# Cross-covariance attention and channel mix on one core: q's root and spread two to three k pieces later in the head, the gated loads one k piece sooner

## The chip, the cores and the metric

The kernel runs on one core of a Trainium2 chip. The time is the device time of one execution in microseconds. It was 508.25 us before the change, the median of four runs (507.77 to 508.81).

## What is computed

Four batches of q, k and v, each 6208 rows by 256 channels in fp32, go through a cross-covariance attention and then through a channel mix. All norms run over the rows, so the attention matrix is only 256 by 256 for each batch:

```
qn = q / (norm(q, axis=1) + 1e-6);  kn = k / (norm(k, axis=1) + 1e-6)
a  = softmax(kn^T @ qn / tau)            # 256 x 256 per batch
x  = v @ a
xk = mu_k * x + (1 - mu_k) * shift(x);   xr = mu_r * x + (1 - mu_r) * shift(x)
out = sigmoid(xr @ w_r) * (relu(xk @ w_k)^2 @ w_v)
```

Here shift moves x down by one row within its batch; w_k is 256 by 1024, w_v 1024 by 256, w_r 256 by 256.

## The kernel before, in words

The 6208 rows of a batch are cut into NB = 12 pieces of 512 rows and a rest of 64 rows (piece 12). The order of all work on every engine is the order in which the program writes it down: each engine takes its own instructions in that order, and an instruction that has to wait holds up all that stand behind it on that engine. DMAs that SyncE (SP) issues form one queue, those that GpSimd (POOL) issues another; the latter also cast fp32 to bf16.

**The head** handles batch 0 alone. The list `order` (L554 to L557) puts q pieces 0 to 7, then q's rest, then k pieces 0 to 3 in turn with q pieces 8 to 11, then k's rest (g = 12), then k pieces 4 to 9; L578 to L582 add k pieces 10 and 11 in halves and quarters.

- A q piece (L125) is loaded by SP, cast to bf16 on DVE (L130), squared on ACT (L132), and PE sums the squares into `nq_ps` (L115), one piece late through `pend` and `flush`. Filler matmuls (L194) follow.
- A k piece (L138) is loaded by SP into one of eight `f` buffers, cast on DVE (L143) into one of six `kb` buffers, squared on ACT (L145), multiplied with the q piece of the same rows into the covariance `s_ps0` on PE (L148, eight matmuls), and then the norms of the piece before are flushed.
- When q's sums are complete, which is behind k's rest, `root` (L154) copies `nq_ps` out of PSUM on DVE (L159) and POOL raises it to the power one half (L161). `inverse` (L164) and `spread` (L173) are six small DVE operations; `broadcast` (L182) is six small matmuls that put q's inverse norms along the free axis of every partition (`bc_ps`). A DVE copy (L570) keeps them as `rq_bc0`. They are used only behind the last k piece (L590), when the softmax of batch 0 begins.
- The loads of later work wait at a gate: POOL copies one column of a k piece's bf16 tile (L572), which has to wait for that piece's cast; behind it on POOL stand the loads of v block 0 (`v_load(0)`, L234), w_k (L574), v blocks 1 and 2, and the first q and k rows of batch 1 (L432).

Which step stands behind which k piece is set by four conditions in the loop over `order`:

```python
            if g == NB:
                nq = root(nq_ps, 2)
            if g == NB - LEAD + 1:
                bc_ps = broadcast(spread(inverse(nq, 2)), "v", bufs=2)
            if g == 8:
                nc.vector.tensor_copy(rq_bc0, bc_ps)
            if g == 8:
                nc.gpsimd.tensor_copy(gate, kt[:, 0, 0:1])
                v_load(0)
```

With NB = 12 and LEAD = 8 these stand behind k's rest, k5, k8 and k8.

**Behind the head** comes k's own root, the softmax of batch 0, PE transposes of v block 0 (L254), fillers, and `x_first` (L269): the matmuls of x for block 0 (`x_ps`, L275), then the PE transposes of v block 1, which need that block's load.

**The body** (L629) runs over 49 blocks of 512 rows in eight steps each. A step holds the up projection of one block (L339, with ACT's relu at L343 and DVE's square at L350), the down projection of the block before (L399), the gate matmuls (L360), x of a later block (L265), the mixing (L307, L318), and a share of the covariance of the next batch (L443, L447, L475 to L487), whose loads POOL issues (L432).

Of the kernel before, what the change touches and what calls it, by code (L numbers as in the profile page):

```python
# [18 lines left out]
def kernel(  # L19
# [21 lines left out]
    NB = N // M  # L41
# [40 lines left out]
    def rows_of(g):  # L82
        return (P, S) if g < NB else (L, 1)
# [5 lines left out]
    LEAD = 8  # L89
# [35 lines left out]
    def q_piece(g, last=False):  # L125
        rows, n = rows_of(g)
        f = head_load(q, 0, g, 0, n)
        qt = pq.tile([P, S, C], BF16, name="qb", tag="b2", bufs=NB + 1)
        qb[g] = qt
        nc.vector.tensor_copy(qt[:rows, :n], f[:rows, :n])  # L130
        sq = pq.tile([P, S, C], BF16, name="hsq", tag="hsq", bufs=5)
        nc.scalar.activation(sq[:rows, :n], f[:rows, :n], AF.Square)  # L132
        flush()
        pend.append((nq_ps, "q", sq, rows, n, last))
        if g < NB:
            filler(FQ, g)

    def k_piece(g, s0, s1, last=False):  # L138
        rows, n = rows_of(g)
        n = s1 - s0  # L140
        f = head_load(k, 0, g, s0, s1)
        kt = pq.tile([P, S, C], BF16, name="kb", tag="kb", bufs=6)
        nc.vector.tensor_copy(kt[:rows, :n], f[:rows, :n])  # L143
        sq = pq.tile([P, S, C], BF16, name="hsq", tag="hsq", bufs=5)
        nc.scalar.activation(sq[:rows, :n], f[:rows, :n], AF.Square)  # L145
        for s in range(n):
            for ih in range(2):
                nc.tensor.matmul(s_ps0[:, ih, :], kt[:rows, s, ih * P:(ih + 1) * P], qb[g][:rows, s0 + s, :],  # L148
                                 start=first("s"), stop=last and s == n - 1, skip_group_check=True)
        flush()  # L150
        pend.append((nk_ps, "k", sq, rows, n, last))
        return kt

    def root(src, n):  # L154
        a = pn.tile([P, 4], F32, name="nrm_a")
        if len(src.shape) == 3:
            nc.vector.tensor_reduce(a[:, :n], src, axis=AX, op=OP.add)
        else:
            nc.vector.tensor_copy(a[:, :n], src)  # L159
        r = pn.tile([P, 4], F32, name="nrm_r")  # L160
        nc.gpsimd.tensor_tensor(r[:, :n], a[:, :n], half[:, :n], op=OP.pow)  # L161
        return r

    def inverse(r, n):  # L164

        nc.vector.tensor_scalar_add(r[:, :n], r[:, :n], 1e-6)
        o = pn.tile([P, 4], F32, name="nrm_o")
        nc.vector.reciprocal(o[:, :n], r[:, :n])
        return o
# [3 lines left out]
    def spread(r):  # L173
        w = pn.tile([P, 3, 2], BF16, name="rw", bufs=1)
        d = pn.tile([P, 2], F32, name="rd", bufs=1)
        nc.vector.tensor_copy(w[:, 0], r[:, :2])
        nc.vector.tensor_tensor(d, r[:, :2], w[:, 0], op=OP.subtract)
        nc.vector.tensor_copy(w[:, 1], d)
        nc.vector.tensor_tensor(w[:, 2], d, w[:, 1], op=OP.subtract)
        return w  # L180

    def broadcast(w, tag, **kw):  # L182
        bc_ps = ps.tile([P, 2, P], F32, name="bc_ps", tag=tag, **kw)
        for h in range(2):
            for u in range(3):
                nc.tensor.matmul(bc_ps[:, h], w[:, u, h:h + 1].to_broadcast([P, P]), ident,
                                 start=h == 0 and u == 0, stop=u == 2, skip_group_check=True)
        return bc_ps.rearrange("p h d -> p (h d)")

    def filler(n, src=0):  # L190

        f_ps = ps.tile([P, M], F32, name="f_ps", tag="v", bufs=2)
        for u in range(n):
            nc.tensor.matmul(f_ps, ident, qb[src].rearrange("p s c -> p (s c)")[:, :M], start=u == 0, stop=u == n - 1)  # L194
# [36 lines left out]
    def v_load(i):  # L231
        b, t = blocks[i]
        v_bf = pq.tile([P, S, C], BF16, name="v_bf", tag="b2", bufs=NB + 1)
        nc.gpsimd.dma_start(v_bf, v[b, t * M:(t + 1) * M, :].rearrange("(s p) c -> p s c", p=P))  # L234
        st[i, "v"] = v_bf
# [312 lines left out]
    def more_rows(n):  # L548
        while pos["load"] < min(len(loads), n):
            group_load(*loads[pos["load"]])  # L550
            pos["load"] += 1
# [6 lines left out]
    for what, g in order:  # L558
        if what == "q":
            q_piece(g, last=g == NB - 1)  # L560
        else:
            kt = k_piece(g, 0, rows_of(g)[1])
            if g < NB - LEAD or g == NB:
                filler(2 if g < NB else 3)
            if g == NB:
                nq = root(nq_ps, 2)
            if g == NB - LEAD + 1:
                bc_ps = broadcast(spread(inverse(nq, 2)), "v", bufs=2)
            if g == 8:
                nc.vector.tensor_copy(rq_bc0, bc_ps)  # L570
            if g == 8:
                nc.gpsimd.tensor_copy(gate, kt[:, 0, 0:1])  # L572
                v_load(0)
                nc.gpsimd.dma_start(w_k_sb, moe_w_k.rearrange("(ko ki) f -> ki ko f", ki=P))  # L574
                v_load(1)
                v_load(2)
                more_rows(1)
# [51 lines left out]
    for i in range(-2, NBLK):  # L629
        for j in range(8):  # L630
# [61 lines left out]
            for u in due.get(T, []):  # L692
                b, g, s = units[u]
# [48 lines left out]
```

## Time and profile before

| | us |
|---|---|
| median of four runs | 508.25 |
| the profiled execution | 507.97 |
| its span, first to last instruction | 506.2 |
| ACT busy | 430.5 |
| POOL busy | 105.2 |

The granted clock of TensorE was 1.000 of full speed. The page gives the busy time of each engine, the span in 40 slices, and the chain of work that ended last. The head fills the first three slices and a little more: up to 38 us the DMA engines move 320 to 387 GB/s, behind it about 200. By the chain, PE carries 82% of the span, DMA 7% and DVE 6%. In rows of time the columns are start, length, engine, line, operation, tiles, shapes and count, and in brackets the idle time before it and what ended that. A row of the chain has start, length, engine, tile and line. A row of windows has the stretch, its length, the busy time (and number) of PE, PE's weight loads, DVE, ACT and POOL, the clock, the share of the DMA engines and GB/s.

### The profile page before, as it was taken

What the parts mean: (1) busy time and instruction counts of PE and PEld (TensorE: products, weight loads), DVE (VectorE), ACT (ScalarE), POOL (GpSimd) and SP (SyncE); (2) the same over time, 40 slices, a digit from 0 to 9 for tenths busy, and PEclk for the clock granted to TensorE, in tenths of its full rate; (3) what the DMA queues carried; (4) which work ended last, traced back from release to release, by engine and by line L of the source; (5) the groups of instructions that cost most, each with busy time, mean ns of one, the idle gap of its engine ahead of it and who ended that gap; (6) DMA issues with size and microseconds to landing.
All of it is one profiled execution on the core that took longest, in us unless ns stands there. A gap on an engine that the chain in (4) does not pass through costs nothing.

```text
span 506.2 us, 9690 instructions
## 1 busy us (share of the span) xinstructions
PE 490.2 (97%) x3644; PEld 339.3 (67%) x3707; DVE 447.6 (88%) x706; ACT 430.5 (85%) x809; POOL 105.2 (21%) x145
## 2 busy tenths in 40 slices
PE   5799999999999999999999999999999999999997
PEld 2474677777676676676677666767666666666675
DVE  3468798999999999999999999999998788887875
ACT  6787999999998998998999899898787777777774
POOL 0047523332521221221342132100121000000000
DMA  8999999999999999899699999953298753424123
GB/s 332 387 320 192 184 202 206 203 208 197 178 165 205 191 196 142 136 171 169 120 179 196 176 199 154 152 130 83 62 155 163 148 103 93 98 76 91 44 84 105
DMA packets 143535, 83.48 MB, mean 165 GB/s; under 512 B 51264, under 2 KB 140032, under 8 KB 143488
## 3 DMA queue, kind: packets, MB, share of 16 engines
q0 software_dynamic: 65808, 33.01, 53.1%
q1 hardware_dynamic: 77536, 49.79, 42.7%
q8 instruction: 29, 0.48, 0.4%
q14 instruction: 18, 0.15, 0.1%
q10 hardware_dynamic: 144, 0.07, 0.0%
HBM read 78.71 MB, written 25.43 MB: 206 GB/s over the span
## 4 chain that ended last, share of the span: by engine, by line
PE 82%; DMA 7%; DVE 6%; ACT 2%; issue 2%; SPq 1%; POOL 0%; ACTq 0%
PE v_ps L399 31%; PE kT_ps L339 28%; PE g_ps L360 9%; PE xT_ps L265 7%; PE s_ps L443 6%; DMA f<-in_q_dram 4%; DMA f<-in_k_dram 2%; DMA v_bf<-in_v_dram 2%; DVE kk L350 1%; DVE acc L481 1%; DVE xk L318 1%; DVE res L412 1%; ACT kr L343 1%; DVE xr L318 1%; PE v_ps L388 1%
## 5 line engine op out<-in xcount | busy, mean ns | idle before, releaser
L343 ACT ACTIVATE kr<-kT_ps 128x512 bf16<-128x512 f32 (+1 forms) x392 | 232.4, 597 | 35.8 <-PE kT_ps L339 27.1
L399 PE MATMUL v_ps<-w_v_sb,kk 128*128 128x256 bf16 x1520 | 228.0, 273 | 0.8
L339 PE MATMUL kT_ps<-xk,w_k_sb 128*128 128x512 bf16 (+1 forms) x721 | 217.3, 377 | 1.2 <-DVE xk L318 0.3
L399 PEld LDWEIGHTS <-kk 128*128 128x128 bf16 x1520 | 148.6, 98 | 57.0
L350 DVE TENSOR_TENSOR kk<-kr 128x1024 bf16<-128x1024 bf16 (+1 forms) x196 | 132.7, 679 | 30.7 <-ACT kr L343 30.1
L447 ACT ACTIVATE sq<-qk 128x512 f32<-128x512 bf16 (+1 forms) x147 | 93.4, 635 | 0.0
L339 PEld LDWEIGHTS <-w_k_sb 128*128 128x128 bf16 x780 | 75.1, 98 | 22.2 <-issue 0.9
L360 PE MATMUL g_ps<-w_r_sb,xr 128*128 128x256 bf16 x388 | 73.6, 273 | 1.4
L267 ACT CAST X<-xT_ps 128x512 bf16<-128x512 f32 x94 | 55.6, 591 | 18.8 <-PE xT_ps L265 18.3
L318 DVE SCALAR_TENSOR_TENSOR xr<-delta,mu_r_t,X 128x512 bf16<-128x512 bf16 x96 | 71.2, 743 | 0.0
L360 PEld LDWEIGHTS <-xr 128*128 128x128 bf16 x388 | 37.9, 98 | 45.2 <-issue 1.3
L318 DVE SCALAR_TENSOR_TENSOR xk<-delta,mu_k_t,X 128x512 bf16<-128x512 bf16 x96 | 67.6, 745 | 0.0
L412 DVE SCALAR_TENSOR_TENSOR res<-res,v_ps 128x512 f32<-128x512 f32 x95 | 64.5, 679 | 0.0
L432 POOL DMA_DIRECT2D qk<-in_q_dram x39 | 28.6, 734 | 157.9 <-ACT sq L447 132.6
L405 ACT ACTIVATE res<-g_ps 128x512 f32<-128x512 f32 x97 | 57.9, 598 | 0.0
L265 PE MATMUL xT_ps<-vT,a_sb 128*128 128x512 bf16 x188 | 55.9, 379 | 0.5 <-ACT vT L258 0.5
L443 PE MATMUL s_ps<-qk 128*128 128x256 bf16 (+1 forms) x294 | 56.1, 272 | 0.0
L481 DVE TENSOR_TENSOR acc<-acc,sq 128x1024 f32<-128x1024 f32 x44 | 53.6, 1217 | 0.1
L234 POOL DMA_DIRECT2D v_bf<-in_v_dram x48 | 37.2, 777 | 61.8 <-DMA vT<-v_bf 40.5
L443 PEld LDWEIGHTS <-qk 128*128 128x128 bf16 (+1 forms) x294 | 27.7, 98 | 12.4 <-issue 1.3
L307 DVE TENSOR_TENSOR delta<-X 128x1024 bf16<-128x1024 bf16 x48 | 32.9, 685 | 0.4 <-ACT X L267 0.3
L432 POOL DMA_DIRECT2D qk<-in_k_dram x39 | 29.0, 744 | 6.5 <-DMA qk<-in_q_dram 2.0
(76 smaller groups left out, 233.4 us busy)
## 6 DMA issues: line engine op xcount, KB each, us to landing
out_dram<-res SPq DMA_DIRECT2D x47, 512.0 KB, 4.4
v_bf<-in_v_dram POOLq DMA_DIRECT2D x48, 256.0 KB, 9.4
qk<-in_q_dram POOLq DMA_DIRECT2D x36, 256.0 KB, 9.3
qk<-in_k_dram POOLq DMA_DIRECT2D x36, 256.0 KB, 10.9
f<-in_q_dram SPq DMA_DIRECT2D x12, 512.0 KB, 8.0
f<-in_k_dram SPq DMA_DIRECT2D x10, 512.0 KB, 8.9
f<-in_k_dram SPq DMA_DIRECT2D x3, 256.0 KB, 7.2
vT<-v_bf SPq DMA_TRANSPOSE x44, 8.6
```

The costliest lines, as they stand in the source:

```text
L265: nc.tensor.matmul(xT_ps, a_sb[:, b, ih, dh * P:(dh + 1) * P], vT[:, :, ih, :], start=ih == 0, stop=ih == 1)
L318: nc.vector.scalar_tensor_tensor(o[:, dh], st[i, "d"][:, dh], mu[:, dh:dh + 1], X[:, dh, c:c + M], op0=OP.mult, op1=OP.add)
L339: nc.tensor.matmul(kT_ps[:, :m], w_k_sb[:, dh, fh * P:(fh + 1) * P], xk[:, dh, :m], start=dh == 0, stop=dh == 1)
L343: nc.scalar.activation(st[i, "kr", fh // 2][:, fh % 2, :m], kT_ps[:, :m], AF.Relu, scale=RH)
L350: nc.vector.tensor_tensor(st[i, "kk"][:, fh - 1:fh + 1, :m], kr[:, :, :m], kr[:, :, :m], op=OP.mult)
L360: nc.tensor.matmul(g_ps[:, s % 2], xr[:, dh, s * P:(s + 1) * P], w_r_sb[:, dh, :], start=s % 2 == 0 and dh == 0, stop=dh == 1, skip_group_ ...
L399: nc.tensor.matmul(v_ps[:, s % 2], kk[:, fh, s * P:(s + 1) * P], w_v_sb[:, fh, :], start=s % 2 == 0 and fh == 0, stop=fh == 7, skip_group_ ...
L405: nc.scalar.activation(st[i, "res"][:, 2 * u:2 * u + 2], st.pop((i, "g", u)), AF.Tanh, scale=0.5)
L412: nc.vector.scalar_tensor_tensor(r, r, 1.0, st.pop((i, "v", u)), op0=OP.add, op1=OP.mult)
L443: nc.tensor.matmul(cov[b][:, ih, :], qk[:rows, s, 1, ih * P:(ih + 1) * P], qk[:rows, s, 0, :], start=g == GORD[0] and s == 0 and ih == 0, ...
L447: nc.scalar.activation(G["sq", s // 2][:rows, s % 2], qk[:rows, s], AF.Square)
L481: nc.vector.tensor_tensor(acc[b], acc[b], G["sq", w - 3], op=OP.add)
```

## The change

Four conditions of the loop change, nothing else. The same instructions are issued on every engine.

```diff
             kt = k_piece(g, 0, rows_of(g)[1])
             if g < NB - LEAD or g == NB:
                 filler(2 if g < NB else 3)
-            if g == NB:
+
+            if g == 5:
                 nq = root(nq_ps, 2)
-            if g == NB - LEAD + 1:
+            if g == 7:
                 bc_ps = broadcast(spread(inverse(nq, 2)), "v", bufs=2)
-            if g == 8:
+            if g == 9:
                 nc.vector.tensor_copy(rq_bc0, bc_ps)
-            if g == 8:
+            if g == 7:
                 nc.gpsimd.tensor_copy(gate, kt[:, 0, 0:1])
                 v_load(0)
                 nc.gpsimd.dma_start(w_k_sb, moe_w_k.rearrange("(ko ki) f -> ki ko f", ki=P))
```

The root stands behind k5 in place of k's rest (k4 and k5 lie between), inverse, spread and broadcast behind k7 in place of k5, the copy to `rq_bc0` behind k9 in place of k8, and the gate with its loads behind k7 in place of k8. On DVE the copy of q's sums comes behind the casts of k4 and k5; the six small operations come between the casts of k7 and k8. On PE the six broadcast matmuls come between the matmuls of k7 and k8. On POOL and SP the order is the same as before.

## The prediction

> **What bounds the kernel now.** I first read the busy table and the wait totals. The row that matters is PE: 490.2 us of a 506.2 us span. From 52 us to the end PE's waits add up to about half a microsecond (one of 0.27 us at 365, the rest 0.05 each), so the body is PE work laid end to end. A change in the head is worth what it takes out of PE's idle time before 52 us, or adds to it, and nothing behind gives it back. So I read PE's own row of time between 27 and 45 us.
>
> ```profile
> PE 490.2 (97%) x3644; PEld 339.3 (67%) x3707; DVE 447.6 (88%) x706; ACT 430.5 (85%) x809; POOL 105.2 (21%) x145
> ...
> 28.19 0.81 PE L194 MATMUL f_ps<-qb,ident 128*128 128x512 bf16 x3
> 29.18 1.05 PE L148 MATMUL s_ps<-qb,kb 128*128 128x256 bf16 x8 [0.18 <-DVE kb L143]
> ...
> 41.39 1.11 PE L275 MATMUL x_ps<-vT,a_sb 128*128 128x512 bf16 x4
> 43.09 0.62 PE L254 MATMUL vT_ps<-ident,v_bf 128*128 128x128 bf16 x8 [0.60 <-DMA v_bf<-in_v_dram]
> ```
>
> Here are two holes that the change can reach: 0.18 us before k piece 4 (PE waits for DVE's cast) and 0.60 us before the transposes of v block 1 (PE waits for that block's load). Matmuls overlap: 128x512 matmuls start 0.215 us apart but are shown 0.38 us long, so the next could have started 0.16 us before the shown end. Against that pace the holes are 0.35 and 0.76 us, together 1.11 us: the most that closing both is worth.
>
> What opens each hole stands in DVE's row of time and in the chain of work that ended last.
>
> ```profile
> 28.37 0.16 DVE L159 COPY nrm_a<-nq_ps 128x2 f32<-128x2 f32 x1 [1.63 <-PE nq_ps L115]
> 28.44 1.28 DVE L143 CAST kb<-f 128x1024 bf16<-128x1024 f32 x2
> 29.80 0.17 DVE L166 TENSOR_SCALAR nrm_r<-nrm_r 128x2 f32<-128x2 f32 x1
> ...
> 30.88 1.29 DVE L143 CAST kb<-f 128x1024 bf16<-128x1024 f32 x2
> 32.34 0.69 DVE L143 CAST kb<-f 128x1024 bf16<-128x1024 f32 x1 [0.18 <-DMA f<-in_k_dram]
> ```
> ```profile
> 32.34 0.70 DVE kb L143
> 33.05 0.06 issue
> 33.10 0.19 POOL gate L572
> 33.29 0.06 issue
> 33.35 1.28 POOL v_bf L234
> 34.62 0.72 POOL w_k_sb L574
> 35.34 7.71 DMA v_bf<-in_v_dram
> 43.05 0.04 issue
> 43.09 0.64 PE vT_ps L254 x8
> ```
>
> The copy of q's norms out of PSUM stood 1.63 us at the front of DVE's queue for PE's last q norms, and the casts of k4 and k5 stood behind it; ACT was already squaring k4 at 27.3 (its row: two squares in 1.47 us from 26.90, the first, 64x256, 0.40 us). The chain says what opens the second hole: cast of k8, gate on POOL, three DMA issues, 7.71 us of transfer. Last I read the half-microsecond windows:
>
> ```profile
> 33.50:34.00 0.50, 0.50 (x13) 0.47 (x12) 0.38 (x1) 0.30 (x1) 0.50 (x1) 1.00 1.03 359
> 34.50:35.00 0.50, 0.50 (x13) 0.47 (x12) 0.35 (x2) 0.50 (x2) 0.50 (x2) 1.00 0.33 53
> 35.00:35.50 0.50, 0.50 (x9) 0.44 (x7) 0.50 (x1) 0.50 (x2) 0.50 (x2) 1.00 0.27 60
> 36.50:37.00 0.50, 0.50 (x13) 0.46 (x12) 0.49 (x2) 0.28 (x2) 0.50 (x2) 1.00 1.44 197
> ```
>
> The last two columns are the DMA engines' share and GB/s. Between the end of the k loads and the start of the gated ones they stand nearly idle for a microsecond.
>
> **Part 1: the root two pieces later.** The copy of nq_ps then stands behind the casts of k4 and k5, and PE's norms are done (28.3) when DVE reaches it (about 29.2): its wait goes. k4's cast can run at 27.3 to 28.0; PE takes up k4 when its three fillers let it, at 28.62 + 0.215 = 28.83 in place of 29.18. Gain 0.35 us. POOL's power (1.15 us) moves with it, to about 29.4 to 30.6, clear of the gate.
>
> **Part 2: inverse, spread and broadcast two pieces later.** The same six small DVE operations (29.80 to 30.96, 1.17 us) and the same six matmuls (0.33 us) are issued; only their place changes. On PE, the matmuls go from before k6 to before k8 and cost the same. On DVE, k6 no longer waits for the six (cast at 29.8 in place of 30.88), but k8 does: k7 lands at 31.1 as now, its cast ends at 31.8, the six end at 32.9, k8's cast at 33.5. PE's order at its own pace, 1.08 us from one k piece to the next (31.71, 32.79, 33.86 in its row), with k4 taken 0.35 us sooner (k4 28.83, k5 29.94, k6 31.03, k7 32.11, norms, broadcast 33.18) asks for k8 at 33.51. So k8's cast lands on the edge: 0 to 0.1 us lost. Without that cover, say with the six or the cast 0.3 us longer, PE waits that 0.3. I take 0.05 and keep 0 to 0.35. The copy to rq_bc0 (0.42 us), one piece later, runs from 34.2 to 34.65 before k10's first half (cast to 35.2); PE asks for that at 35.7: free, with 0.5 us in hand.
>
> **Part 3: gate and loads one piece sooner.** The gate follows k7's cast (31.8) and not k8's (33.04): 1.2 us sooner, after a 0.06 us hop and 0.19 us, with v0 issued at about 32.1. It issues the same DMAs: v0, w_k, v1, v2 and two of qk, 0.55 to 1.28 us each, 4.6 us to 37.95 now and to 36.7 then; k's own root on POOL (38.77) is not behind them in either. v1 landed at 43.05; in a first-in-first-out stream that fills an idle microsecond it lands at about 41.85. PE's x_ps ends, by part 1 and 2, 0.3 us sooner and is free at 42.33 - 0.3 = 42.03. The second hole closes entirely, with 0.15 us to spare.
>
> Two rules of the Trainium skill speak against part 3. The page "SBUF — State Buffer", section "SBUF: two separate sides", says that a DMA issued from GpSimd gets its descriptors from cores that share an SBUF port pair with DVE, and that a DVE fp32 copy in its two-port mode shuts them out for its whole length. The trace fits: v0's issue took 1.28 us across k9's cast, against 0.73 to 0.79 for the next three, and the half-size casts beside POOL's issues took 0.611 us in the mean where a full one takes 0.690. By the rows, the new place swaps the cast of k9 for that of k8 beside the first issues, and nothing changes; by the rule at its worst, one more full cast (0.69 us) shuts out the issues, v1 lands at 42.5, the transposes start at 42.55 and the whole gain is 0.54 us; a cast stretched by 0.2 us also makes k8 late by that. I take 0.1 us of loss for it, nearer the rows. The page "DMA: Bandwidth & Descriptors", section "Issuing engines are not separate DMA queues", says that transfers of all issuers run on the same 16 engines and interleave, so v0's start would delay the last k pieces. The windows say how much: v0's first full microsecond after its start moved about 0.06 MB, which at k's 400 GB/s is 0.15 us; k's last piece was cast by 36.99 and PE took it at 38.03, will want it at 37.7. Covered by 0.7 us: nothing.
>
> **What is late next.** DVE's queue behind x_first moves by only 0.3 us plus its idle of 0.2 and 0.35 us there, so the second xk of block 1 comes some 0.9 us sooner; but ACT's chain, which PE waits for at 51.74 (0.22 us for vT), moves by the full gain of the transposes. Also w_v (landing near 50.8, first used at 51.03) moves with the stream by about 1.1 us. So 0.9 to 1.1 us pass.
>
> **Sum.** 0.35 + 0.76 - 0.05 - 0.1 = 0.96, taken as 0.95 us. The profiled execution (507.97 us: span 506.2 and 1.77 around it) would become 507.0; the median of the runs shown, 508.25, lies 0.28 above that, so the forecast is 507.3. A difference of 0.2% (1.02 us) is about what a measurement of this kernel can tell from no change, and the forecast lies at that border.
>
> **Rivals.**
> A, as summed: both holes close, -0.75 to -1.15 us, 507.3. Chance 0.55; the part beyond 1.02 us gets 0.24, the rest 0.31.
> B, more than the holes: PE's later small waits (0.23 at 44.81, 0.22 at 51.74) shrink as well because loads run ahead of their users. 0.95 + 0.45 = 1.4, so 506.85. For it: both waits are on ACT copies of v blocks. Against it: those copies start from PE's transposes and move with them. Chance 0.22, counted as faster.
> C, the release does not do what it says: v1 is held by the issues or by the stream's rate, not by its start. Then the second hole only moves; part 1 gives 0.3 us at most and the hole eats it, since v1 lands as before: 508.2. Against it: the idle microsecond in the windows. Chance 0.08, no change.
> D, slower: the sooner stream meets k's tail. Now the gated stream needs 1.7 us from issue to its first packets and so begins after k. If, issued at 32.1, it is in the mix at 33.0, about 0.5 MB of k is still to be moved; at half of the mixed rate (190 GB/s) that takes 5.2 us, k's last piece lands 3.3 us later, PE's last k matmuls come 2.3 us later (1.0 us of slack is used up first), and x_first ends at 42.33 + 2.3, which is 1.5 us behind the 43.09 of now: 509.75. It decides once k's last cast moves from 36.99 to beyond 38.8. Chance 0.15.
>
> So faster 0.24 + 0.22 = 0.46, no change 0.31 + 0.08 = 0.39, slower 0.15. The range takes in A, B and C and stops short of most of D: 506.5 to 508.7.
>
> **What would show it.** In the profile after: the copy of nq_ps waits for nothing and k4's s_ps starts near 28.85; no wait for a cast above 0.1 us before k8; gate near 31.9; the idle microsecond in the windows gone; the transposes of v1 start near 42.1 with no wait for a DMA. It is wrong if k11's casts end after 38, if PE waits for v1 still, or if a new wait before 60 us stands in PE's row.

## The result and the profile after

The changed kernel takes 507.87 us (median of 42 runs) against 508.45 us for the kernel before (60 runs). The ratio is 0.9989 (95% interval 0.9985 to 0.9993): a gain of 0.56 us, between about 0.36 and 0.76. It is clear of the noise, but it lies inside the 0.2% that the prediction takes as the border of no change, and it is 0.4 us less than the 0.95 us forecast. The profiled execution took 508.17 us with a span of 506.4. That is slower than the profiled execution of before (507.97, span 506.2), so the gain of the medians can't be read off this one pair.

The PE row of the busy table and PE's rows of time, after:

```profile
PE 489.8 (97%) x3644; PEld 339.4 (67%) x3707; DVE 447.5 (88%) x706; ACT 430.2 (85%) x809; POOL 105.2 (21%) x145
```
```profile
27.86 0.35 PE L115 MATMUL nq_ps<-ones_b,hsq 128*128 128x1 bf16 x8
28.07 0.81 PE L194 MATMUL f_ps<-qb,ident 128*128 128x512 bf16 x3
28.71 1.04 PE L148 MATMUL s_ps<-qb,kb 128*128 128x256 bf16 x8
...
33.05 0.65 PE L186 MATMUL bc_ps<-ident,rw 128*128 128x128 bf16 x6
33.90 1.05 PE L148 MATMUL s_ps<-qb,kb 128*128 128x256 bf16 x8 [0.21 <-DVE kb L143]
...
41.44 1.10 PE L275 MATMUL x_ps<-vT,a_sb 128*128 128x512 bf16 x4
42.97 0.62 PE L254 MATMUL vT_ps<-ident,v_bf 128*128 128x128 bf16 x8 [0.43 <-DMA v_bf<-in_v_dram]
```

The first hole is closed: from the start of the last q norms to k4 it is 0.85 us, where it was 1.20 (27.98 to 29.18). A new hole stands further down: from the broadcast to k8 it is 0.85 us, where the broadcast before took PE 0.33 us (31.38 to 31.71). So x_ps is where it was (41.44, before 41.39). The hole before v1's transposes is 0.43 us, where it was 0.60.

DVE's rows of the same stretch, after:

```profile
29.25 0.15 DVE L159 COPY nrm_a<-nq_ps 128x2 f32<-128x2 f32 x1
...
32.17 0.17 DVE L176 CAST rw<-nrm_o 128x2 bf16<-128x2 f32 x1
32.38 0.16 DVE L177 TENSOR_TENSOR rd<-nrm_o,rw 128x2 f32<-128x2 f32 x1
32.57 0.47 DVE L178 CAST rw<-rd 128x2 bf16<-128x2 f32 x1
33.08 0.16 DVE L179 TENSOR_TENSOR rw<-rd,rw 128x2 bf16<-128x2 f32 x1
33.16 1.43 DVE L143 CAST kb<-f 128x1024 bf16<-128x1024 f32 x2
```

The copy of q's sums waits for nothing. But the second cast of the spread (L178), two elements a partition, takes 0.47 us where it took 0.17. POOL's rows say what lies beside it:

```profile
31.93 0.18 POOL L573 COPY gate<-kb 128x1 bf16<-128x1 bf16 x1 [1.32 <-DVE kb L143]
32.17 0.91 POOL L234 DMA_DIRECT2D v_bf<-in_v_dram  x1
33.08 0.91 POOL L575 DMA_DIRECT2D w_k_sb<-in_moe_w_k_dram  x1
```

The gate fell at 31.93, 1.17 us sooner. L178 ended 0.03 us before v0's issue did (33.08). The chain of work that ended last, same stretch:

```profile
32.17 0.91 POOL v_bf L234
33.08 0.90 POOL w_k_sb L575
33.98 8.94 DMA v_bf<-in_v_dram
42.97 0.63 PE vT_ps L254 x8
```

The issue of v1 starts 1.36 us sooner than before (33.98, before 35.34), but from there to its landing it is 8.94 us instead of 7.71: v1 lands at 42.92, 0.13 us sooner. The half-microsecond windows show what the stream of gated loads met:

```profile
34.50:35.00 0.50, 0.50 (x14) 0.47 (x12) 0.50 (x3) 0.50 (x2) 0.50 (x2) 1.00 1.29 192
35.00:35.50 0.50, 0.50 (x11) 0.45 (x8) 0.50 (x2) 0.50 (x3) 0.50 (x1) 1.00 1.10 154
35.50:36.00 0.50, 0.50 (x11) 0.46 (x10) 0.50 (x2) 0.50 (x3) 0.50 (x2) 1.00 1.44 167
36.00:36.50 0.50, 0.50 (x14) 0.45 (x11) 0.50 (x2) 0.50 (x3) 0.50 (x2) 1.00 1.42 98
36.50:37.00 0.50, 0.50 (x13) 0.47 (x11) 0.42 (x2) 0.47 (x3) 0.23 (x1) 1.00 0.57 52
37.00:37.50 0.50, 0.50 (x10) 0.45 (x9) 0.00 (x0) 0.34 (x1) 0.00 (x0) 1.00 0.94 105
```

The microsecond at shares 0.33 and 0.27 is gone, but the DMA engines are now busy with little to show for it (share 1.42 at 98 GB/s) and a dip follows at 36.5. Summed over these six windows, GB/s times 0.5 us, 0.38 MB were moved; in before it was 0.37 MB in the same three microseconds, with the gate a microsecond later.

### The profile page after: what moved, and what is told of

It is laid out like the page before. It is cut to its first block, busy times and chain, and to the rows that moved or that the text cites. A ratio compares the mean times of both kernels' runs of the same rounds, so it can differ in the third digit from the quotient of the medians.

```text
span 506.4 us, 9691 instructions
## 1 busy us (share of the span) xinstructions
PE 489.8 (97%) x3644; PEld 339.4 (67%) x3707; DVE 447.5 (88%) x706; ACT 430.2 (85%) x809; POOL 105.2 (21%) x145
## 4 chain that ended last, share of the span: by engine, by line
PE 83%; DVE 6%; DMA 5%; issue 2%; ACT 2%; SPq 1%; POOL 0%; ACTq 0%
PE v_ps L399 31%; PE kT_ps L339 28%; PE g_ps L360 9%; PE xT_ps L265 7%; PE s_ps L443 6%; DMA f<-in_q_dram 2%; DMA f<-in_k_dram 2%; DMA v_bf<-in_v_dram 2%; DVE kk L350 1%; DVE acc L481 1%; DVE xk L318 1%; DVE res L412 1%; PE s_ps L148 1%; ACT kr L343 1%; DVE xr L318 1%
```

## The experiments

The expectations name four theories. **P**: the root and spread moves are worth nothing in the end, all gain is the gate's. **L**: POOL's issues and DVE's operations hold each other up where they lie side by side. **M**: the loads of mu_k and mu_r (SP, right behind k's last piece; 1 KB each in 256 packets of four bytes) sit on the DMA engines just where the sooner stream arrives. **R**: v1 is bound by POOL's issues or by the stream's own rate, whatever else runs. All ratios are to the kernel before on the same chip, with 95% intervals.

### Each half alone

The gate alone, from the kernel before:

```diff
-            if g == 8:
+            if g == 7:
                 nc.gpsimd.tensor_copy(gate, kt[:, 0, 0:1])
```

> The kernel before with the gate and its loads behind k7 in place of k8, nothing else. The six spread operations then stand behind k5 and are over before POOL issues. Theory M (the 4-byte packets of the two mu loads share the DMA engines with the sooner stream): v1 lands only 0.1 to 0.3 us sooner than the 43.05 us of before, total -0.1 to -0.3 us. Rival L (the shared port of DVE and POOL: issue and spread hold each other up): no spread beside the issues, so v1 lands 1 us sooner and the total is -0.6 to -0.8 us.

> The gate alone once more, beside the kernel after on the same chip. Theory P (the root's and spread's move is worth nothing because its gain is lost again at k8; all of the change is the gate): the same time as the kernel after within 0.3 us, or up to 0.4 us faster. Rival: both halves count, the kernel after is 0.4 us or more faster.

Measured, the same kernel twice: 507.4 us, 0.9984 (0.9976 to 0.9992), and 507.9 us, 0.9995 (0.9985 to 1.0006); only the first is clear of the noise. Against its expectation the first is mixed: v1 landed at 42.72, near what M said, and the time fell by some 0.8 us, as L said. The order alone, the changed kernel with its gate put back:

```diff
-            if g == 7:
+            if g == 8:
                 nc.gpsimd.tensor_copy(gate, kt[:, 0, 0:1])
```

> The kernel after with the gate and its loads back behind k8. Theory L for the first half (in the profile after, one of the six spread operations took 0.47 in place of 0.17 us beside v0's issue): without an issue beside it the spread takes 1.17 us again, PE takes k8 at about 33.6 in place of 33.90 and x_ps comes 0.25 us sooner; v1 lands as before at 43.05, so the transposes do not move and the total is 0 to -0.1 us against before. Rival (k8 is late because it is cast behind the spread at all): k8 at 33.9 again, and the same total.

Measured: 508.43 us, 0.9999 (0.9991 to 1.0008). The changed kernel itself was run again with the later sets:

> The kernel after once more, for a second profile. Theory M (mu's 4-byte packets share the engines with the gated stream and hold up the slowest ones): v0's first engine lands near 36.2 us but its last 1.5 us or more later, v1's last near 42.9, the transposes within 0.2 us of before. Rival (the one profile was a chance): v1's last landing moves by over 0.4 us from 42.92.

> The kernel after a third time, beside the next three on the same chip. From the runs so far: 0.4 to 1.0 us under before; one more profile for the landing of v1 (42.9 and 43.1 us in the two so far).

Measured: 507.71 us, 0.9974 (0.9963 to 0.9986), where the runs of before were scattered (507.7 to 512.6, median 509.01), and 507.64 us, 0.9987 (0.9978 to 0.9996).

So the gate alone gives 0.05% and 0.16%, both halves 0.11%, 0.13% and 0.26%, the order alone nothing that shows. That fits P, though the interval of the order alone leaves room for a gain of up to 0.09%, some 0.45 us. Why the order is worth so little is seen in the rows. First DVE and then PE of the order-only kernel, where no POOL issue lies beside the spread:

```profile
32.73 0.17 DVE L178 CAST rw<-rd 128x2 bf16<-128x2 f32 x1
32.93 0.16 DVE L179 TENSOR_TENSOR rw<-rd,rw 128x2 bf16<-128x2 f32 x1
```
```profile
28.15 0.35 PE L115 MATMUL nq_ps<-ones_b,hsq 128*128 128x1 bf16 x8
...
33.34 0.49 PE L186 MATMUL bc_ps<-ident,rw 128*128 128x128 bf16 x6
33.76 1.05 PE L148 MATMUL s_ps<-qb,kb 128*128 128x256 bf16 x8
...
41.30 1.11 PE L275 MATMUL x_ps<-vT,a_sb 128*128 128x512 bf16 x4
43.59 0.62 PE L254 MATMUL vT_ps<-ident,v_bf 128*128 128x128 bf16 x8 [1.18 <-DMA v_bf<-in_v_dram]
```

The cast is back at 0.17 us, k8 waits for nothing, and the way from the broadcast to k8 is 0.42 us: 0.09 over the 0.33 of before. From the last q norms to x_ps it is 13.15 us, against 13.41 in before: the order alone does give 0.26 us. It is then waited away (1.18 us for v1, which lands at 43.54). With the sooner gate the same way is 13.58 and 13.48 us in two profiles of the changed kernel, and 13.36 with the mu loads doubled (below). In the changed kernel's remaining profile, the second, it is 15.02 us, for another reason: v0 itself landed at 39.28 (37.95 in before), and PE waited for it.

```profile
39.33 0.62 PE L254 MATMUL vT_ps<-ident,v_bf 128*128 128x128 bf16 x8 [0.98 <-DMA v_bf<-in_v_dram]
```

There x_ps came at 42.38, and v1, landed at 43.11, held up nothing.

L178 was 0.47 or 0.48 us in all seven profiles (the experiments below among them) that have the sooner gate and the spread behind k7, and in each it ended 0.03 us before v0's issue did. The profile of before held such casts too, far behind the head, where the spread of a later batch meets issues of POOL that follow one another without a gap. A row of DVE and the row of POOL beside it:

```profile
137.85 0.51 DVE L178 CAST rw<-rd 128x2 bf16<-128x2 f32 x1
137.60 0.77 POOL L234 DMA_DIRECT2D v_bf<-in_v_dram  x1
```

Over all fourteen profiles, the 91 casts of this form that began 0.25 to 0.41 us into an issue of POOL took 0.43 to 0.52 us, and each ended at most 0.04 us before the issue did. The 14 without an issue beside them took 0.17 us, and so did the 7 that began together with one. The loss is shown to come with the issue beside it, which is L. That the engine was held for a port is not shown: the profiles show the length of the cast and the common end.

### Do the loads of mu hold v1?

Left out, with constants in their place, from the changed kernel and from the kernel before:

```diff
+    nc.vector.memset(mu_k_t, 0.5)
+    nc.vector.memset(mu_r_t, 0.5)
...
-    nc.sync.dma_start(mu_k_t, moe_mu_k.rearrange("(h p) -> p h", p=P))
-    nc.sync.dma_start(mu_r_t, moe_mu_r.rearrange("(h p) -> p h", p=P))
```

> The kernel after without the two loads of mu (they are set to 0.5 by DVE at the start; the loads are left out). Theory M: without their 4-byte packets the gated stream runs at its full rate from the start, v1 lands near 41.9 us in place of 42.92, the wait of 0.43 us before its transposes goes, the transposes start near 42.4 and the total is 0.5 to 0.6 us under the kernel after. Rival R (the stream is bound by POOL's issues or by its own rate): v1 lands at 42.7 to 42.9 and the total is that of the kernel after.

> The kernel before without the two loads of mu (set to 0.5 by DVE). Theory M: there the 4-byte packets ran in the idle stretch from 34 to 36 us, before the gated stream, so leaving them out changes next to nothing: v1 at 42.9 to 43.05, total 0 to -0.1 us. If leaving them out is worth as much here as in the kernel after, theory M is wrong about what the sooner gate met.

Measured: 507.72 us, 0.9987 (0.9979 to 0.9995), and 508.64 us, 1.0009 (1.0001 to 1.0017). The windows of the first:

```profile
34.50:35.00 0.50, 0.50 (x13) 0.46 (x12) 0.50 (x3) 0.50 (x2) 0.50 (x2) 1.00 1.24 211
35.00:35.50 0.50, 0.50 (x7) 0.44 (x6) 0.45 (x2) 0.50 (x2) 0.50 (x1) 1.00 1.39 219
35.50:36.00 0.50, 0.50 (x13) 0.47 (x11) 0.47 (x2) 0.50 (x2) 0.50 (x2) 1.00 1.42 229
36.00:36.50 0.50, 0.50 (x13) 0.46 (x10) 0.50 (x2) 0.50 (x2) 0.50 (x2) 1.00 1.14 201
36.50:37.00 0.50, 0.50 (x13) 0.45 (x11) 0.34 (x2) 0.50 (x3) 0.15 (x1) 1.00 1.18 200
37.00:37.50 0.50, 0.50 (x10) 0.46 (x8) 0.00 (x0) 0.17 (x1) 0.00 (x0) 1.00 1.11 196
```

The same shares now carry about 200 GB/s throughout: 0.63 MB in place of 0.38. v1 landed at 41.85, PE's transposes of it start at 42.21 with no wait, 0.76 us sooner than in the changed kernel, and yet the time is that of the changed kernel. A part of what took the gain is in PE's rows (this kernel's lines stand two lower):

```profile
42.21 0.61 PE L256 MATMUL vT_ps<-ident,v_bf 128*128 128x128 bf16 x8
...
45.80 0.38 PE L341 MATMUL kT_ps<-xk,w_k_sb 128*128 128x512 bf16 x1 [0.19 <-DVE xk L320]
```

PE now waits for DVE's xk at 45.80, and v_ps follows at 50.70, 0.20 us sooner than in the changed kernel (50.90). Past 64 us the work stands 0.43 us sooner; why the medians show none of this, the profile does not say. Without the mu loads but with the late gate (e4) v1 lands at 43.13: there they cost v1 nothing that shows, as its issue (35.34 in before) comes when their last packets (35.96) are nearly through.

Doubled, two more such loads behind the first two, from the changed kernel:

```diff
+    mu_x = [const.tile([P, 2], F32, name="mu_x%d" % u) for u in range(2)]
+    nc.sync.dma_start(mu_x[0], moe_mu_k.rearrange("(h p) -> p h", p=P))
+    nc.sync.dma_start(mu_x[1], moe_mu_r.rearrange("(h p) -> p h", p=P))
```

> The kernel after with both mu loads issued twice, the second time into tiles that nothing reads. Theory M: twice the 4-byte packets beside the gated stream, so v1 lands 0.4 to 1.0 us later (43.3 to 43.9) and the total is 0.4 to 0.9 us above the kernel after. Rival R (the stream is bound by its own rate or by POOL): no change, v1 at 42.9.

Measured: 508.53 us, 0.9991 (0.9978 to 1.0004); v1 landed at 42.83, no later than in the changed kernel, though the two added loads landed at 40.94 and 42.63, beside w_k and v1. M in its simple form, the more packets the later, fell here.

Loaded as two rows of 1 KB (no four-byte packets) and turned by four small fp32 matmuls before the fillers, from the changed kernel and from the gate-only one:

```diff
-    nc.sync.dma_start(mu_k_t, moe_mu_k.rearrange("(h p) -> p h", p=P))
-    nc.sync.dma_start(mu_r_t, moe_mu_r.rearrange("(h p) -> p h", p=P))
+    nc.sync.dma_start(mu_row[:, 0], moe_mu_k.rearrange("(o c) -> o c", o=1))
+    nc.sync.dma_start(mu_row[:, 1], moe_mu_r.rearrange("(o c) -> o c", o=1))
...
+            nc.tensor.matmul(mu_ps[:, u, h:h + 1], mu_row[:, u, h * P:(h + 1) * P], one_f,
```

> The kernel after with each mu loaded as one row of 1 KB into one partition, at the same place on SP, and turned by four small matmuls and two small copies behind the v0 transposes. Theory M (mu's 512 four-byte packets beside the gated stream cost it a microsecond on the engines): v1 lands at 41.8 to 42.1 us, no wait before its transposes, 0.3 to 0.6 us under the kernel after. Rival R (they cost nothing that PE feels): within 0.15 us of the kernel after.

> The gate alone (behind k7, root and spread where they were before) with mu loaded as rows. Theory M: v1 lands near 42.0 and the total is 0.2 to 0.5 us under the gate alone. If P holds too, it is within 0.3 us of the run with both halves and mu as rows.

Measured: 508.26 us, 1.0005 (0.9997 to 1.0013), and 508.66 us, 1.0007 (0.9999 to 1.0015). v1 landed at 41.54 and 41.40. The turning cost time of its own, as one row of PE in the first shows:

```profile
38.74 1.05 PE L604 MATMUL mu_ps<-one_f,mu_row 1*128 1x1 f32 x8
```

Four tiny matmuls (eight records) took 1.05 us in PE's way, and x_ps started at 42.32. The total time of these two kernels therefore tells nothing about M; v1's landing may. All profiles but those of the two kernels further down, whose head runs about a microsecond later, by the bytes moved from 34.0 to 37.5 us (sum of the windows) and v1's landing:

| gate | mu's four-byte packets | kernel | MB | v1 lands |
|---|---|---|---|---|
| k8 | yes | before | 0.49 | 43.05 |
| k8 | yes | order only | 0.48 | 43.54 |
| k8 | none | no mu, before | 0.50 | 43.13 |
| k7 | yes | changed, three profiles | 0.51, 0.50, 0.63 | 42.92, 43.11, 42.19 |
| k7 | yes | gate only, two profiles | 0.59, 0.67 | 42.72, 41.48 |
| k7 | yes | mu twice | 0.46 | 42.83 |
| k7 | none | no mu | 0.77 | 41.85 |
| k7 | none | mu as rows, two kernels | 0.78, 0.69 | 41.54, 41.40 |

Behind the sooner gate every kernel of the table without the four-byte packets moved more (0.69 to 0.78 MB) than any with them (0.46 to 0.67), and landed v1 by 41.85, as only one of the six others did. That speaks for M, with 0.18 MB between the means (0.74 against 0.56). Three things speak against taking it as shown. The gate alone, with the same packets, landed v1 at 42.72 and at 41.48. These two profiles come from two chips, and the chip is a rival that the runs do not part from M: on the chip of the 41.48, the two row kernels landed v1 at 41.54 and 41.40 and the changed kernel at 42.19. And the two kernels further down have the sooner gate and no such packets beside it either; from the gate to v1's landing they took 10.71 and 11.07 us, against 9.47 to 10.10 in the three kernels without packets above and 9.21 to 11.74 in the six profiles with them. So the packets may be a part of it, and what makes the rest is open. R in its plain form falls: two profiles of the same chip that issued v1 at 34.14 (the third of the changed kernel, the second of the gate alone) landed it 0.71 us apart, and the stream could run at 200 GB/s where it ran at 98.

### Taking mu out of the way, and the spread too

The mu loads issued by ACT at the very start of the changed kernel:

```diff
     omu = const.tile([P, 2], F32, name="omu")
+    nc.scalar.dma_start(mu_k_t, moe_mu_k.rearrange("(h p) -> p h", p=P))
+    nc.scalar.dma_start(mu_r_t, moe_mu_r.rearrange("(h p) -> p h", p=P))
...
-    nc.sync.dma_start(mu_k_t, moe_mu_k.rearrange("(h p) -> p h", p=P))
-    nc.sync.dma_start(mu_r_t, moe_mu_r.rearrange("(h p) -> p h", p=P))
```

> The kernel after with the mu loads issued from ACT's queue at the very start. Theory M: the gated stream meets only k's tail, v1 lands near 42.0 us, the transposes start behind x_ps with no wait, and the total is 0.3 to 0.5 us under the kernel after (0.8 to 1.0 under before), less what the 512 small packets cost the first q loads (0 to 0.3). Rival R: v1 at 42.9 and the total of the kernel after or up to 0.3 more.

Measured: 509.19 us, 1.0004 (0.9991 to 1.0016), 1.5 us above the changed kernel of the same set. A miss: the small packets were said to cost the first q loads at most 0.3 us. SP's row of the first q loads, in this kernel and then in the changed one:

```profile
0.74 7.89 SPq L100 DMA_DIRECT2D f<-in_q_dram  x9
```
```profile
0.74 5.49 SPq L98 DMA_DIRECT2D f<-in_q_dram  x9
```

The nine issues stretch from 5.49 to 7.89 us, and the last q norms come at 29.45 where they came at 27.86. On top of it the spread and broadcast are put behind the last k piece, clear of the issues of v0 and w_k, and the copy to `rq_bc0` behind the copy of k's norms:

```diff
-            if g == 7:
-                bc_ps = broadcast(spread(inverse(nq, 2)), "v", bufs=2)
...
+    rw0 = spread(inverse(nq, 2))
     flush()
+    bc_ps = broadcast(rw0, "v", bufs=2)
```

> The run with mu first, and inverse, spread and broadcast moved behind the last k piece's cast, the copy to rq_bc0 behind the copy of k's norms. Theory (the gain of the root's move is lost at k8, which is cast behind the spread): no wait before k8, x_ps 0.3 to 0.4 us sooner than with mu first alone, the xk of the next blocks sooner by the same, total 0.3 us lower still (1.1 to 1.3 under before). Rival (the broadcast now lies on the way to the softmax): exp starts 0.3 us later, no gain or a loss of 0.3.

Measured: 509.56 us, 1.0013 (1.0001 to 1.0025). x_ps started at 42.95, against 43.04 without the move, and PE waited 0.33 us for a k cast instead of 0.21 before k8. From the last q norms (28.98 here) to x_ps it is 13.97 us, against 13.59 without the move. The thought that the spread's place between casts was the last thing in the way of the head fell: without it PE meets another late cast.

## Why the prediction was right, and where its steps were not

The sign and the range were right, and the gate fell and moved v1 in the direction said. The size was 0.56 in place of 0.95 us, and three terms of the sum did not come as said. That the time still fell inside the range owes as much to its width as to the argument: 506.5 to 508.7 us also holds the 508.45 us of the kernel before, and no change within 0.2% was given a chance of 0.39, behind the 0.46 of a larger gain. Of the signs named for being wrong, two came: PE still waited for v1, 0.43 us in this profile, and in another it met a new wait before 60 us. Before k8 PE waited 0.21 us for a cast, where at most 0.1 was said.

**Part 1, the root later: right.** 0.35 us was said for the first hole, and 1.20 less 0.85 is 0.35. The copy waits for nothing and k4 starts at 28.71 (28.85 was said).

**Part 2 and the rule on the shared port: the term was too small.** "0 to 0.1 us lost ... I take 0.05" and "0.1 us of loss", together 0.15 (and a range of 0 to 0.35 for the first), against 0.85 less 0.33 = 0.52 us in the changed kernel's profile and 0.47 and 0.42 in the others of it. Of the 0.52, 0.30 us is the longer cast and 0.09 is lost in the order-only kernel too; the rest, 0.13, is that the spread itself stood later against PE (L178 began 4.71 us behind the last q norms, 4.58 in the order-only kernel). The rule of the Trainium skill, page "SBUF — State Buffer", section "SBUF: two separate sides", had been read mainly one way: DVE shutting POOL's issues out. The section calls the pair a lock that whoever starts first keeps, so it works the other way too, for a DVE operation in a two-port mode; whether this cast is in one, no run shows. The rows fall that way for L178, which ended with v0's issue: 33.05 and 33.08 here, 33.21 and 33.24, 32.49 and 32.53 in the other two profiles of the changed kernel. They do not for k8's cast, which began at 33.16, 0.08 us into w_k's issue, and took its usual 0.69 us. The two halves of the change were costed one by one: part 2 moved the small operations to 31.77 to 33.24, part 3 moved v0's issue to 32.17 to 33.08, and no step laid these two intervals side by side. The large casts were weighed against the issues, the six small operations were not, though the profile of before shows such a cast at 0.51 us beside an issue (at 137.85). So part 1's gain came and went: from the last q norms to x_ps 0.26 us was kept in the order-only kernel and 0.07 to 0.17 lost in the two profiles of the whole one in which v0 was not late.

**Part 3, the gate: on time, but "the idle microsecond" was not idle.** The gate was said for 31.9 and came at 31.93, and the k loads did not suffer (their last cast ended at 36.95, before at 36.99), so rival D did not happen. v1 was said for 41.85 and came at 42.92 in this profile. The low share was a mean over engines that finish at different times: in before the last quarter of k landed at 34.56 on the first DMA engine and at 36.28 on the last. v0's first engine finished 1.26 us sooner than before (36.16, was 37.42), its last not at all (38.03, was 37.95). In the second profile of the changed kernel v0's last engine came 1.33 us later than before (39.28), and PE waited for that; the prediction asked only when v1 lands, not whether v0 suffers. What the late engines still had in hand was k's tail and the four-byte packets, of which the last ran to 37.35. The prediction's 1.7 us from v0's issue to its first packets was short as well: 1.98 us in before (33.35 to 35.33) and 2.02 after. In the page's rows of DMA issues the mu loads take 5.4 and 5.4 us to land after the change, 4.4 and 4.1 before. By the table, v1 landed at 42.54 in the mean of the six profiles with the gate at k7 and the four-byte packets, and at 43.24 in the mean of the three with the gate at k8: 0.70 us sooner, not 1.2.

**What is late next: w_v did not move.** The prediction let w_v's landing go "with the stream by about 1.1 us". Its issue stands on POOL behind k's root, at 41.68 before and 41.74 after, and it landed at 50.55 (50.8 was read) and 50.41. With its first use at 51.03 that left only some 0.5 us of cover. Two profiles in which v1 was early show it; PE's rows of another profile of the changed kernel, and of the gate alone:

```profile
42.54 0.61 PE L254 MATMUL vT_ps<-ident,v_bf 128*128 128x128 bf16 x8
...
51.53 0.49 PE L399 MATMUL v_ps<-w_v_sb,kk 128*128 128x256 bf16 x3 [0.74 <-DMA w_v_sb<-in_moe_w_v_dram]
```
```profile
42.35 0.61 PE L254 MATMUL vT_ps<-ident,v_bf 128*128 128x128 bf16 x8
...
50.69 0.49 PE L399 MATMUL v_ps<-w_v_sb,kk 128*128 128x256 bf16 x3
```

In the first the second hole is closed as forecast, 0.93 us from x_ps to the transposes, and PE then waits 0.74 us for w_v, landed at 51.49. In the second w_v landed at 50.65, 0.04 us ahead of its use.

**The body passes everything on: right.** The first cast of X past 64 us and those up to 487 us differ from before by one constant within 0.02 us in each profile: -0.12 in the changed kernel's first, +0.15 and +0.12 in its others, -0.32 and -0.72 for the gate alone, +0.50 for the order alone. The ends of the spans add up to 0.66 us of their own to these. In ten of these thirteen further profiles (all but that of before) this constant is, within 0.03 us, what v1's transposes had moved; the other three are the one that waited for w_v and two in which PE waited for xk. The mean of the six profiles with the sooner gate and the mu packets is -0.18 (mu twice: -0.20), of the three with the late gate +0.20 (no mu, before: +0.09): 0.38 us apart.

**Open:** where the 0.56 us lies. The three profiles of the changed kernel stand at +0.05 us in the mean, so they show no gain, and their executions took 0.30 to 0.58 us more than the medians of their runs (508.17, 508.29 and 508.11 against 507.87, 507.71 and 507.64). The gain is put down to the gate by the runs of the halves alone. Open too is why v1's landing varies by over a microsecond, and how the packets of mu act. In the changed kernel's three profiles v1 landed the later the later mu_r did (36.87, 37.72 and 39.80 us for 42.19, 42.92 and 43.11), but the two of the gate alone do not follow that (36.37 and 36.75 for 42.72 and 41.48), and more packets did not go with a later v1. No variant is shown to be faster than the changed kernel.

## What to carry to other kernels

When a change moves two things, lay the new places of both over one time axis on all engines: two moves that are each free can meet. Look for the same operation elsewhere in the profile: its cost beside other work may already be there. A low mean share of the DMA engines need not be room for a load; ask which engine ends last, and what happens to the first load of the stream as well as to the one that is waited for. Before a closed hole is counted, look up the next load's issue and what it stands behind, since a load that doesn't move caps the gain.

## What the runs showed of the hardware

- A DVE cast of two elements a partition that began 0.25 to 0.41 us into a DMA issue of POOL took 0.43 to 0.52 us and ended with the issue (91 of 91, in fourteen profiles); without an issue, or begun together with one, it took 0.17 us (21 of 21).
- With two loads of 1 KB in four-byte packets issued by ACT at the start, nine issues of SP took 7.89 and 8.26 us (two kernels) in place of 5.39 to 5.65 (the changed kernel's three profiles), and the last q norms came at 29.45 and 28.98 in place of 27.36 to 28.13.
- Four fp32 matmuls of one column (eight records) took 1.05 us of PE, in two kernels.
- One v load behind the same gate landed at 42.72 and at 41.48 us in two executions of one kernel, on two chips; on one chip, with v1 issued at 34.14 both times, two kernels landed it 0.71 us apart.
- The last quarter of k landed on the sixteen DMA engines over 1.72 us, from 34.56 on the first to 36.28 on the last.
